# A raw-weight buffer that outlives attention, two weight pieces read early, and plan costs set to measured times

## The chip, the cores and the metric

The kernel runs on one core of a Trainium2 chip. A core has five engines that run their own instruction lists and wait for each other by semaphores: TensorE (PE in the profile, its weight loads PEld), VectorE (DVE), ScalarE (ACT), GpSimd (POOL) and SyncE (SP), which issues most DMAs. The metric is the device time of one execution in microseconds (us). Before the change it was 739.23 us, the median of three runs (738.7 to 740.27).

## The reference

Three parts follow each other. The first is attention over 2 x 8 heads of 768 tokens by 64, in which a query sees only the keys of its own bucket; the bucket is the sign pattern of six random projections. The second is a dense layer over 1536 tokens, and the third sends each token to one of eight experts, 192 tokens each, in the order of the gate's scores.

```python
mask = q_bucket[:, :, :, None] == k_bucket[:, :, None, :]
scores = np.where(mask, scale * q @ k.T, -1e9)     # softmax, then @ v
...
h = x @ w_in                                       # x 1536x512, w_in 512x2048
g = np.maximum(h, 0.0) + alpha * np.minimum(h, 0.0)
x = g @ w_out                                      # w_out 2048x512
...
h = np.maximum(x[mask] @ w1[e], 0.0)               # 192 tokens of each expert
out[mask] = h @ w2[e]
```

w_in and w_out come in 64-bit floating point; every other input is 32-bit.

## The kernel before

**Stages.** Attention fills TensorE until about 225 us. The dense layer, called moe1 in the code, follows until about 530 us and shares its end with the routing of tokens; the experts run until the end. The input of the dense layer, xT, is attention's output transposed, and it has a high part xh and a low part xl, since every product of moe1 is done as three matmuls on rounded halves (low weight by high input, high by low, high by high).

**Weights.** A piece of w_in or w_out is 128 x 512 numbers of 64 bits, read by SyncE as raw words into a buffer of 128 x 1024 words (tile wraw, 512 KB). `turn` makes it usable in five steps: VectorE builds 32-bit numbers in a PSUM bank (tile pscv) in three instructions, b1 (L602), b2 (L605) and b3 (L608); ScalarE copies them to the high half (L613); VectorE subtracts to get the low half (L614). The third step gives the raw buffer back. w_in has 16 pieces, of which 12 are read and turned during attention, and w_out has 16, one for each f below, all of them read and turned in moe1. Two raw buffers, each of one piece, are used in attention; they belong to the pool `stg`, which is closed with attention. moe1 opens two others in its own pool, and reads its four w_in pieces into the space of the next block's input before that is made (tile wx).

**moe1.** Four blocks of 384 tokens, and in each 16 rounds f. A round has twelve matmuls of the first product into the bank psh (L699 to L701); the relu with slope, two passes on ScalarE (L718, L720) and one on VectorE (L722, tile gt); a rounded copy gh on ScalarE (L926) and its remainder gl on GpSimd or VectorE (L930); and twelve matmuls of the second product into the bank psy (L728 to L730), which read gh, gl and the wout halves of f. The high and low part of the next block's input (x_ops, L669 and L672) are made during the block before.

**The order of the work.** Every stage collects its operations in a `Plan`, each with its engine or engines, a cost in us, a priority (a due time), what it comes after, and which buffers of a ring it takes and gives. `Plan.order` simulates engines with these costs, takes at every step the operation that could start first, with the priority as a small weight, and so writes each engine's instruction list once, when the kernel is built. On the chip each engine runs its list in that order. The list therefore depends on the costs and on the constants at the head of the file. Each engine waits in place: if an instruction is not ready, nothing behind it on that engine goes ahead.

**The experts.** For each expert, TensorE picks its tokens' numbers (rp<-tt, L1315), VectorE turns them to an index (L1318), GpSimd issues two gathers (L1383) and the fetches of w1 and w2 (L1365), TensorE transposes the gathered rows (L1413) and makes the products, and GpSimd scatters the results (L1500).

Of the kernel before, what the change touches and what calls it, by code (L numbers as in the profile page):

```python
# [7 lines left out]
F32 = mybir.dt.float32  # L8
# [4 lines left out]
U32 = mybir.dt.uint32  # L13
# [11 lines left out]
XP = 10.89  # L25
RP = 11.53
RB = 19.57
PK0 = -119.54
PK = -106.32
NPL = 4  # L30
NB = 384
# [6 lines left out]
WA = -6.05  # L38
XA = -32.34
TA = 20.0  # L40
TB = 1.5
YA = 0.74
RD = 2.82
HC = 1
HOT = 0
NWA = 12
IN0 = 4.6
IA = -7.85
# [113 lines left out]
class Attn:  # L162
# [353 lines left out]
    def run(s):  # L516
        s.setup()
        s.o_x = {}
        pl = aplan()
        for h in range(2 * NH):  # L520
            s.head(h, pl, h * 6 * SL)
        for i in range(NWA):
            s.m.w_in_ops(pl, i, PO["w"] + i * PO["dw"])
        s.m.consts_ops(pl, s, s.o_x[2])
        s.m.bank0 = s.bank
        pl.emit(s.warm, 1.0, WEND)


class Moe:
# [19 lines left out]
    def consts_ops(s, pl, at, o):  # L549

        nc = s.nc
        T = {}

        def load():
            T["a"] = s.stg.tile([16, 128], F32, name="al16", bufs=1)
            nc.sync.dma_start(out=T["a"], in_=s.alpha.rearrange("(f p) -> f p", p=128))
            nc.sync.dma_start(out=s.wg[:, :, 0:8], in_=s.w_gate.rearrange("(p k) e -> p k e", p=128))

        def tr():
            T["p"] = at.bank("psal")  # L560
            nc.tensor.transpose(T["p"][:, 0:16], T["a"], s.ident[0:16, 0:16])

        def cp():
            nc.vector.tensor_scalar(s.al, T["p"][:, 0:16], -1.0, None, op0=OP.mult)

        o = pl.op({"SP": 1.2}, load, 0.0, [o], dma=0.4)
        o = pl.op({"PE": 0.2}, tr, 0.0, [o], ["B"])
        pl.op({"DVE": 0.1}, cp, 0.0, [o], (), ["B"])
# [8 lines left out]
    def f64_load(s, src):  # L577
        t = s.stg.tile([128, 512, 2], U32, name="wraw", bufs=2)
        s.nc.sync.dma_start(out=t.rearrange("p n two -> p (n two)"), in_=src.bitcast(U32))
        return t  # L580

    def w_in_ops(s, pl, i, at):

        nc = s.nc
        j, k = divmod(i, 4)
        T = {}

        def load():
            T["raw"] = s.f64_load(s.w_in[k * 128:(k + 1) * 128, j * 512:(j + 1) * 512])

        hi, lo = s.wih[j][:, k], s.wil[j][:, k]
        o = pl.op({"SP": 0.45}, load, at, take=["wr"], dma=1.46)
        s.turn(pl, T, o, ["B"], ["wr"], lambda n: s.bank0(n), lambda: hi, lambda: lo, lambda x: at + 3 + x)

# [29 lines left out]
    def w_ops(s, pl, n, src, parts, at, pr, own):  # L624

        nc = s.nc
        T = {}
        bank = ("OA", "OB")[n % 2]

        def load():  # L630
            if own:
                raw = s.xb[1].tile([128, 1536], U32, name="wx", tag=("xh", "xl")[s.nx % 2])[:, 0:1024]
                s.nx += 1
            else:
                raw = s.yp.tile([128, 1024], U32, name="wraw", tag="wr", bufs=2)
            T["raw"] = raw.rearrange("p (n two) -> p n two", two=2)
            nc.sync.dma_start(out=raw, in_=src.bitcast(U32))

        o = pl.op({"SP": 0.45}, load, pr(at - 2.0), take=["XR" if own else "WR"], dma=1.46)
        return s.turn(pl, T, o, [bank], ["XR" if own else "WR"], lambda name: s.bank(name, bank), *parts, lambda x: pr(at + x))  # L640
# [20 lines left out]
    def x_ops(s, pl, blk, k, after, at, w, take=()):  # L661
# [12 lines left out]
        o = pl.op({"ACT": 0.41}, hi, at, after, take)  # L674
        return pl.op({"DVE": 0.47, "POOL": 0.96} if blk else {"DVE": 0.47}, lambda e="DVE": lo(e), at + 0.4 * w, [o])

    def x_init(s, cl):
        s.cl = cl
        s.xb = [cl.enter_context(s.tc.tile_pool(name="xb0", bufs=1))]
        s.xh, s.xl, s.o_xl = {}, {}, {}  # L680
# [66 lines left out]
    def moe1(s, pl, r):  # L747
# [3 lines left out]
        T = {}  # L751
# [37 lines left out]
        def out(e, blk, k):  # L789
            if k % 2 == 0:  # L790
                T["yt", blk] = s.yp.tile([128, 2, NB], F32, name="yt", tag="wr", bufs=2)
# [46 lines left out]
        def wog_ops():  # L838
# [33 lines left out]
            for q in range(4):  # L872
                o_t = []
                for k in range(4):
                    at = (TA + (4 * q + k) * TB) * U
                    o_l = op({"SP": 0.45}, lambda q=q, k=k: load(q, k), at - 2 * U, o_x[1], ["RAW"], dma=1.46)
                    for n, t in enumerate((0.34, 0.6, 0.6)):
# [22 lines left out]
        for blk in range(4):  # L900
# [4 lines left out]
            for f in range(16):  # L905
# [22 lines left out]
                def lo(e, blk=blk, f=f):  # L928
# [3 lines left out]
                for k in range(4):  # L932
                    o_h = [op({"PE": 0.49}, lambda k=k, h=h: h(k), at + 0.1 * k, [o_x[blk][k]] if blk else [o_i[x] for x in (f // 4 * 4 + k,) if x in o_i], [ring] if k == 0 else [],
                              ["X"] if f == 15 and k == 3 and blk < 2 else [], o_h)]
                b = blk < 3
                o = op({"ACT": 0.41}, a1, at + 1.0, o_h, ["GT", "G"] if b else ["GR"], behind=o_free if blk == 3 else [])
                o = op({"ACT": 0.41}, a2, at + 1.1, [o])
                o = op({"DVE": 0.47}, a3, at + 1.15, [o], (), [ring])
                o_a = o
                o = op({"ACT": 0.41}, hi, at + 1.2, [o])  # L940
                o_gl = op({"DVE": 0.85, "POOL": 1.0}, lo, at + 1.3, [o], (), ["GT"] if b else [])
                if b:
                    at = (i + LAG) * U + 0.5
                    for k in range(4):
                        o_y[blk, f, k] = op({"PE": 0.49}, lambda blk=blk, f=f, k=k: y(blk, f, k), at + 0.1 * k,
# [42 lines left out]
        for k in range(4):  # L988
            for f in range(16):
                o = [op({"PE": 0.49}, lambda f=f, k=k: y(3, f, k), at, o_y[3, f], ["L"] if f == 0 else [],  # L990
# [529 lines left out]
def body(ctx, tc, q, k, v, proj, w_in, w_out, alpha, w_gate, w1, w2, cst, w_out_t, out):  # L1520
# [11 lines left out]
    m.x_init(cl)  # L1532
    with ExitStack() as c2:
        m.stg = c2.enter_context(tc.tile_pool(name="stg", bufs=2))
# [56 lines left out]
```

## Time and profile before

| what | value |
|---|---|
| runs | 738.7, 739.23, 740.27 us (median 739.23) |
| the profiled execution | 736.62 us, of which the span on the core is 734.5 us |
| TensorE busy | 709.9 us, 97% of the span |
| VectorE, ScalarE, GpSimd busy | 448.9, 311.3, 257.7 us |
| mean granted clock of TensorE | 0.991 of full speed |

The profile is of one execution, so sums are made against its 736.62 us, which is 2.61 us below the median of the runs. The page lists the busy time of every engine, then the waits by line; a window of the trace gives busy time in a stretch, with the granted clock (1.00 is 2.4 GHz, 0.50 is 1.2 GHz) and the share of time in which the DMA engines worked. In a timeline row the bracket at the end gives the idle time before that instruction on its engine, and the instruction or transfer that ended it. A queue of SyncE is marked SPq.

### The profile page before, as it was taken

The numbers are of one execution on the slowest core, as the hardware profiler recorded it, in microseconds if no ns is written. First come the engines' busy times: TensorE is split into PE (matmuls) and PEld (weight loads), VectorE is DVE, ScalarE is ACT, GpSimd is POOL, SyncE is SP. The second block draws the span as 40 slices with busy tenths as digits, with TensorE's granted clock in tenths as the row PEclk, the third lists the DMA queues.
The fourth block names the chain that finished last, engine by engine and source line by source line (L and its number), as shares of the span: only waits on it lengthen the run. The fifth ranks groups of instructions, "written<-read, shape, count | busy, mean of one in ns | idle before, by whom it ended". The sixth has DMA issues, their size and how long they took to land. (4 is left out here: it accounts for less than half of the span.)

```text
span 734.5 us, 14803 instructions
## 1 busy us (share of the span) xinstructions
PE 709.9 (97%) x6062; PEld 602.2 (82%) x6062; DVE 448.9 (61%) x989; ACT 311.3 (42%) x569; POOL 257.7 (35%) x220
## 2 busy tenths in 40 slices
PE   7999999999988799999999999999999999999996
PEld 6888888888887699999999999898978667666662
DVE  4888988888976989724454533456667565551000
ACT  4677787778743444633353333541021111112110
POOL 2498888889761121100000000005243413323101
PEclk9999999999999999999999999999999999999999
DMA  8455665655205455130223200200667546539201
GB/s 226 99 138 139 152 172 131 175 138 138 45 2 172 141 174 174 37 97 29 87 65 127 86 1 1 76 2 1 217 256 296 220 174 231 200 144 376 98 7 37
DMA packets 33091, 93.27 MB, mean 127 GB/s; under 512 B 4448, under 2 KB 17920, under 8 KB 30720
## 3 DMA queue, kind: packets, MB, share of 16 engines
q1 hardware_dynamic: 28016, 52.08, 24.8%
q0 software_dynamic: 4688, 39.85, 14.8%
q8 instruction: 48, 0.79, 0.4%
q10 hardware_dynamic: 320, 0.40, 0.2%
q14 instruction: 19, 0.16, 0.1%
HBM read 71.86 MB, written 8.65 MB: 110 GB/s over the span
## 5 line engine op out<-in xcount | busy, mean ns | idle before, releaser
L440 POOL TENSOR_TENSOR pl<-p 128x768 f16<-128x768 f32 (+1 forms) x94 | 134.5, 1449 | 35.6 <-ACT p L432 35.4
L334 DVE TENSOR_REDUCE m<-psm 128x1 bf16<-128x768 f32 x96 | 89.8, 956 | 13.9 <-PE psm L328 12.5
L432 ACT ACTIVATE p<-pss 128x768 f32<-128x768 f32 (+1 forms) x98 | 76.4, 797 | 40.2 <-PE pss L426 30.9
L699 PE MATMUL psh<-xh,win 128*128 128x384 f32 x256 | 87.9, 343 | 1.6 <-ACT xT L505 0.9
L701 PE MATMUL psh<-xh,win 128*128 128x384 f32 x256 | 85.9, 335 | 0.0
L700 PE MATMUL psh<-xl,win 128*128 128x384 f32 x256 | 85.7, 335 | 0.0
L930 POOL TENSOR_TENSOR gl<-gt,gh 128x384 fp32r<-128x384 f32 x18 | 19.1, 1066 | 171.4 <-ACT gh L926 169.7
L729 PE MATMUL psy<-gh,wout 128*128 128x384 f32 x192 | 65.2, 340 | 2.8 <-DVE wout L614 2.8
L728 PE MATMUL psy<-gl,wout 128*128 128x384 f32 x192 | 65.9, 343 | 2.0 <-ACT wout L613 2.0
L451 PE MATMUL av<-v,pl 128*128 128x65 f16 x576 | 63.5, 195 | 2.4 <-DVE xt L489 2.4
L730 PE MATMUL psy<-gh,wout 128*128 128x384 f32 x192 | 65.0, 338 | 0.0
L1471 PE MATMUL oa<-xw,ht 128*128 128x512 f32 x128 | 64.7, 598 | 0.0
L722 DVE SCALAR_TENSOR_TENSOR gt<-psh,al,gt 128x384 f32<-128x384 f32 x48 | 29.5, 615 | 55.4 <-ACT psh L720 55.3
L451 PEld LDWEIGHTS <-pl 128*128 128x128 f16 x576 | 53.9, 100 | 11.1 <-issue 11.0
L452 PE MATMUL av<-v,p 128*128 128x65 f16 x576 | 63.1, 195 | 0.0
L453 PE MATMUL av<-v,p 128*128 128x64 f16 x576 | 62.8, 195 | 0.0
L1439 PEld LDWEIGHTS pl<-xg,xw 128*128 128x128 f32 x256 | 42.1, 190 | 19.0 <-issue 18.2
L718 ACT ACTIVATE gt<-psh 128x384 f32<-128x384 f32 x48 | 23.6, 492 | 78.7 <-PE psh L701 78.7
L1439 PEld LDWEIGHTS pl<-xT,xw 128*128 128x128 f32 x256 | 41.9, 190 | 16.8 <-issue 14.6
L424 PE MATMUL pss<-Q,K 128*128 128x384 f32 x192 | 54.8, 364 | 0.9 <-ACT p L432 0.8
L699 PEld LDWEIGHTS psh<-xh,win 128*128 128x128 f32 x256 | 48.1, 188 | 8.2 <-issue 6.1
L452 PEld LDWEIGHTS <-p 128*128 128x128 bf16 x576 | 54.1, 99 | 0.1
(237 smaller groups left out, 1660.8 us busy)
## 6 DMA issues: line engine op xcount, KB each, us to landing
K<-Q SPq DMA_DIRECT2D x45, 192.0 KB, 2.9
wraw<-in_moe_w_out_dram SPq DMA_DIRECT2D x16, 512.0 KB, 3.6
xT<-in_moe_w_out_t_dram SPq DMA_DIRECT2D x16, 512.0 KB, 3.6
wraw<-in_moe_w_in_dram SPq DMA_DIRECT2D x12, 512.0 KB, 4.4
vf<-in_v_dram SPq DMA_DIRECT2D x16, 192.0 KB, 4.2
qk<-in_q_dram SPq DMA_DIRECT2D x15, 192.0 KB, 3.3
qk<-in_k_dram SPq DMA_DIRECT2D x15, 192.0 KB, 3.5
Q<-Q SPq DMA_DIRECT2D x15, 192.0 KB, 3.8
```

Source lines behind the costliest of these rows:

```text
L334: nc.vector.tensor_reduce(T["m"][:, t:t + 1], T["mx", t][:, :, 0:384], axis=AX.XY, op=OP.max, negate=True)
L432: nc.scalar.activation(T["p", c].rearrange("p (a n) -> p a n", a=2)[:, x], T["s", c][:, x, 0:384], AF.Exp, scale=0.125)
L440: (nc.vector if eng == "DVE" else nc.gpsimd).tensor_tensor(T["l", c][:, x], p[:, x], T["h", c][:, x], op=OP.subtract)
L451: nc.tensor.matmul(o[:, t, 0:65], lo[:, sl], vt[:, 0:65], start=(c == 0 and t == 0), stop=False, **kw)
L452: nc.tensor.matmul(o[:, t, 0:65], ph[:, sl], vt[:, 0:65], start=False, stop=False, **kw)
L699: nc.tensor.matmul(o, wl[:, k, ff], s.xh[blk][:, k], start=(k == 0), stop=False)
L700: nc.tensor.matmul(o, wh[:, k, ff], s.xl[blk][:, k], start=False, stop=False)
L701: nc.tensor.matmul(o, wh[:, k, ff], s.xh[blk][:, k], start=False, stop=(k == 3))
L728: nc.tensor.matmul(o, wh, gl, start=first, stop=False, skip_group_check=True)
L729: nc.tensor.matmul(o, wl, gh, start=False, stop=False, skip_group_check=True)
L730: nc.tensor.matmul(o, wh, gh, start=False, stop=last, skip_group_check=True)
L1439: nc.tensor.matmul(T["h", j // 2][:, j % 2], w1[:, k, j * 128:(j + 1) * 128], T["xg"][:, k], start=(k == 0 and j % 2 == 0), stop=(k == 3), ...
```

## The change

The pool `stg` with its two raw buffers is opened with the input blocks and closed with them, in place of being closed with attention. moe1 uses these two buffers in place of two of its own, and so do the tiles yt that carry outputs of the dense layer. A small tile al16 moves to attention's own pool. The new `w_out_early` reads the first two pieces of w_out within attention's plan, and moe1 takes these two as already loaded (`got`). Besides, the costs in moe1's plan rise to measured times: the high and low part of x, the turns of the gate weights, the matmul groups, the relu's passes, gh and gl, and the remainders gl of block 0 go only to GpSimd. Eleven constants that set priorities change too; two of them are shown.

```diff
-PK0 = -119.54
...
+PK0 = -80.645
...
-XA = -32.34
...
+XA = 75.008
...
             s.m.w_in_ops(pl, i, PO["w"] + i * PO["dw"])
+        for f in range(2):
+            s.m.w_out_early(pl, f, PO["w"] + (NWA + f) * PO["dw"])
         s.m.consts_ops(pl, s, s.o_x[2])
...
-            T["a"] = s.stg.tile([16, 128], F32, name="al16", bufs=1)
+            T["a"] = at.sm.tile([16, 128], F32, name="al16", bufs=1)
...
-        t = s.stg.tile([128, 512, 2], U32, name="wraw", bufs=2)
+        t = s.stg.tile([128, 512, 2], U32, name="wraw", tag="wr")
...
         s.turn(pl, T, o, ["B"], ["wr"], lambda n: s.bank0(n), lambda: hi, lambda: lo, lambda x: at + 3 + x)
+
+    def w_out_early(s, pl, f, at):
+
+        def load():
+            s.pre[f] = s.f64_load(s.w_out[f * 128:(f + 1) * 128, :])
+
+        pl.op({"SP": 0.45}, load, at, take=["wr"], dma=1.46)
 
...
             else:
-                raw = s.yp.tile([128, 1024], U32, name="wraw", tag="wr", bufs=2)
+                raw = s.stg.tile([128, 1024], U32, name="wraw", tag="wr")
             T["raw"] = raw.rearrange("p (n two) -> p n two", two=2)
...
 
-        o = pl.op({"SP": 0.45}, load, pr(at - 2.0), take=["XR" if own else "WR"], dma=1.46)
+        def got():
+            T["raw"] = s.pre[n]
+
+        if n < 2 and not own:
+            o = pl.op({"IN": 0.0}, got, pr(at - 2.0), take=["WR"])
+        else:
+            o = pl.op({"SP": 0.45}, load, pr(at - 2.0), take=["XR" if own else "WR"], dma=1.46)
         return s.turn(pl, T, o, [bank], ["XR" if own else "WR"], lambda name: s.bank(name, bank), *parts, lambda x: pr(at + x))
...
 
-        o = pl.op({"ACT": 0.41}, hi, at, after, take)
-        return pl.op({"DVE": 0.47, "POOL": 0.96} if blk else {"DVE": 0.47}, lambda e="DVE": lo(e), at + 0.4 * w, [o])
+        o = pl.op({"ACT": 0.5}, hi, at, after, take)
+        return pl.op({"DVE": 0.54, "POOL": 1.1} if blk else {"DVE": 0.54}, lambda e="DVE": lo(e), at + 0.4 * w, [o])
 
...
         s.xb = [cl.enter_context(s.tc.tile_pool(name="xb0", bufs=1))]
-        s.xh, s.xl, s.o_xl = {}, {}, {}
+        s.xh, s.xl, s.o_xl, s.pre = {}, {}, {}, {}
 
...
-                T["yt", blk] = s.yp.tile([128, 2, NB], F32, name="yt", tag="wr", bufs=2)
+                T["yt", blk] = s.stg.tile([128, 2, NB], F32, name="yt", tag="wr")
...
-                    for n, t in enumerate((0.34, 0.6, 0.6)):
+                    for n, t in enumerate((0.45, 0.7, 0.75)):
...
-                def lo(e, blk=blk, f=f):
+                def lo(e="POOL", blk=blk, f=f):
...
-                    o_h = [op({"PE": 0.49}, lambda k=k, h=h: h(k), at + 0.1 * k, [o_x[blk][k]] if blk else [o_i[x] for x in (f // 4 * 4 + k,) if x in o_i], [ring] if k == 0 else [],
+                    o_h = [op({"PE": 0.52}, lambda k=k, h=h: h(k), at + 0.1 * k, [o_x[blk][k]] if blk else [o_i[x] for x in (f // 4 * 4 + k,) if x in o_i], [ring] if k == 0 else [],
...
-                o = op({"ACT": 0.41}, a1, at + 1.0, o_h, ["GT", "G"] if b else ["GR"], behind=o_free if blk == 3 else [])
-                o = op({"ACT": 0.41}, a2, at + 1.1, [o])
-                o = op({"DVE": 0.47}, a3, at + 1.15, [o], (), [ring])
+                o = op({"ACT": 0.48}, a1, at + 1.0, o_h, ["GT", "G"] if b else ["GR"], behind=o_free if blk == 3 else [])
+                o = op({"ACT": 0.48}, a2, at + 1.1, [o])
+                o = op({"DVE": 0.56}, a3, at + 1.15, [o], (), [ring])
...
-                o = op({"ACT": 0.41}, hi, at + 1.2, [o])
-                o_gl = op({"DVE": 0.85, "POOL": 1.0}, lo, at + 1.3, [o], (), ["GT"] if b else [])
+                o = op({"ACT": 0.5}, hi, at + 1.2, [o])
+                o_gl = op({"DVE": 0.55, "POOL": 1.1} if blk else {"POOL": 1.1}, lo, at + 1.3, [o], (), ["GT"] if b else [])
...
-                        o_y[blk, f, k] = op({"PE": 0.49}, lambda blk=blk, f=f, k=k: y(blk, f, k), at + 0.1 * k,
+                        o_y[blk, f, k] = op({"PE": 0.52}, lambda blk=blk, f=f, k=k: y(blk, f, k), at + 0.1 * k,
...
-                o = [op({"PE": 0.49}, lambda f=f, k=k: y(3, f, k), at, o_y[3, f], ["L"] if f == 0 else [],
+                o = [op({"PE": 0.52}, lambda f=f, k=k: y(3, f, k), at, o_y[3, f], ["L"] if f == 0 else [],
...
+    m.stg = cl.enter_context(tc.tile_pool(name="stg", bufs=2))
...
-        m.stg = c2.enter_context(tc.tile_pool(name="stg", bufs=2))
```

SyncE's queue in attention's last heads, before; K and Q are head 14's and head 15's halves, copied from one buffer to another.

```order
L302 DMA Q_3619<-Q_3618 64x768
L302 DMA K_3877<-Q_3879 64x768
L302 DMA K_3878<-Q_3879 64x768
L302 DMA K_3878<-Q_3880 64x768
L302 DMA Q_3880<-Q_3879 64x768
L637 DMA wraw<-in_moe_w_out_dram 128x1024 x2
L637 DMA wx<-in_moe_w_in_dram 128x1024 x2
L637 DMA wraw<-in_moe_w_out_dram 128x1024 x2
```

The same place after the change, where L581 is the early load.

```order
L302 DMA Q_3619<-Q_3618 64x768
L581 DMA wraw<-in_moe_w_out_dram 128x1024
L302 DMA K_3879<-Q_3881 64x768
L302 DMA K_3880<-Q_3881 64x768
L302 DMA K_3880<-Q_3882 64x768
L302 DMA Q_3882<-Q_3881 64x768
L581 DMA wraw<-in_moe_w_out_dram 128x1024
L646 DMA wx<-in_moe_w_in_dram 128x1024 x2
L646 DMA wraw<-in_moe_w_out_dram 128x1024 x2
L646 DMA wx<-in_moe_w_in_dram 128x1024 x2
```

The first early load stands between the last move of one head and the first move of the next; the second stands behind head 15's last move. The two wraw loads that opened moe1 are gone from that place, and 12 of them stand in a row later.

VectorE's list at the end of attention and the start of moe1, before; the first row is attention's last.

```order
L489 TENSOR_TENSOR xt<-av,r 128x6x64
L722 SCALAR_TENSOR_TENSOR gt<-psh,al,gt 128x384
L602 TENSOR_SCALAR pscv<-wraw 128x512
L605 SCALAR_TENSOR_TENSOR pscv<-wraw,pscv 128x512
L608 SCALAR_TENSOR_TENSOR pscv<-wraw,pscv 128x512
L602 TENSOR_SCALAR pscv<-wraw 128x512
L722 SCALAR_TENSOR_TENSOR gt<-psh,al,gt 128x384
L614 TENSOR_TENSOR wout_4582<-pscv,wout_4582 128x512
L605 SCALAR_TENSOR_TENSOR pscv<-wraw,pscv 128x512
L602 TENSOR_SCALAR pscv<-wx 128x512
L608 SCALAR_TENSOR_TENSOR pscv<-wraw,pscv 128x512
```

And after; L611, L614, L617 and L623 are the four steps b1, b2, b3 and the low half, and L737 is the relu.

```order
L489 TENSOR_TENSOR xt<-av,r 128x6x64
L611 TENSOR_SCALAR pscv<-wraw 128x512 x2
L614 SCALAR_TENSOR_TENSOR pscv<-wraw,pscv 128x512 x2
L617 SCALAR_TENSOR_TENSOR pscv<-wraw,pscv 128x512 x2
L737 SCALAR_TENSOR_TENSOR gt<-psh,al,gt 128x384
L623 TENSOR_TENSOR wout_4585<-pscv,wout_4585 128x512 x2
L611 TENSOR_SCALAR pscv<-wx 128x512
L737 SCALAR_TENSOR_TENSOR gt<-psh,al,gt 128x384
L614 SCALAR_TENSOR_TENSOR pscv<-wx,pscv 128x512
L611 TENSOR_SCALAR pscv<-wx 128x512
L617 SCALAR_TENSOR_TENSOR pscv<-wx,pscv 128x512
```

All three steps of both w_out pieces have moved in front of the first relu; the low halves stand behind it, and then the w_in pieces (wx).

ScalarE's list from attention's last copy, before: gh for the first round is the fourth row.

```order
L505 ACTIVATE xT<-psx 128x768
L718 ACTIVATE gt<-psh 128x384
L720 ACTIVATE psh<-psh 128x384
L926 ACTIVATE gh<-gt 128x384
L718 ACTIVATE gt<-psh 128x384
L720 ACTIVATE psh<-psh 128x384
L718 ACTIVATE gt<-psh 128x384
L613 ACTIVATE wout_4582<-pscv 128x512
L720 ACTIVATE psh<-psh 128x384
L926 ACTIVATE gh<-gt 128x384
```

And after; L733 and L735 are the relu's passes, L622 is a high half and L941 is gh.

```order
L505 ACTIVATE xT<-psx 128x768
L733 ACTIVATE gt<-psh 128x384
L735 ACTIVATE psh<-psh 128x384
L733 ACTIVATE gt<-psh 128x384
L622 ACTIVATE wout_4585<-pscv 128x512 x2
L941 ACTIVATE gh<-gt 128x384
L735 ACTIVATE psh<-psh 128x384
L733 ACTIVATE gt<-psh 128x384
L941 ACTIVATE gh<-gt 128x384
L735 ACTIVATE psh<-psh 128x384
```

The two high halves of wout now stand before the first gh, and the second round's first relu pass before both. TensorE's list, in the same place, has 36 matmuls of the first product ahead of the first group of the second, where it had 42.

## Rows read from the trace of the kernel before

**Rows 1.** The page: busy time, share of the span and instructions of TensorE

```profile
PE 709.9 (97%) x6062; PEld 602.2 (82%) x6062; DVE 448.9 (61%) x989; ACT 311.3 (42%) x569; POOL 257.7 (35%) x220
```

**Rows 2.** Windows: per engine busy us, instructions; then granted clock, DMA share

```profile
240.00:260.00 20.00, 15.16 (x77) 14.08 (x76) 19.85 (x35) 9.66 (x21) 2.78 (x3) 0.94 0.46 148
300.00:400.00 100.00, 100.00 (x603) 94.78 (x602) 47.15 (x84) 40.88 (x87) 3.41 (x3) 1.00 0.26 81
540.00:640.00 100.00, 100.00 (x699) 68.64 (x698) 59.88 (x216) 17.21 (x34) 34.74 (x28) 1.00 0.64 235
```

**Rows 3.** Waits of TensorE in 225 to 500: total us, times, longest

```profile
PE psy L729 <- DVE wout L614: 2.8, 2, 2.0
PE psy L728 <- ACT wout L613: 2.0, 2, 1.2
...
PE psh L699 <- DVE gt L722: 0.7, 1, 0.7
```

**Rows 4.** Timeline of TensorE: start, duration, engine, line, tiles, idle before

```profile
245.38 0.44 PE L729 MATMUL psy<-gh,wout 128*128 128x384 f32 x1 [0.78 <-DVE wout L614]
...
257.50 0.66 PE L729 MATMUL psy<-gh,wout 128*128 128x384 f32 x1 [2.04 <-DVE wout L614]
...
261.08 0.33 PE L699 MATMUL psh<-xh,win 128*128 128x384 f32 x1
...
261.95 0.34 PE L701 MATMUL psh<-xh,win 128*128 128x384 f32 x1
```

**Rows 5.** Windows: five us of the first layer

```profile
255.00:260.00 5.00, 2.91 (x9) 2.69 (x10) 4.95 (x10) 2.19 (x6) 0.00 (x0) 0.76 0.67 211
```

**Rows 6.** Timeline of ScalarE, VectorE and GpSimd where the first layer begins

```profile
224.62 0.81 ACT L505 ACTIVATE xT<-psx 128x768 f32<-128x768 f32 x1 [4.92 <-PE psx L500]
...
228.83 0.62 DVE L722 SCALAR_TENSOR_TENSOR gt<-psh,al,gt 128x384 f32<-128x384 f32 x1 [5.24 <-ACT psh L720]
...
229.95 0.49 ACT L718 ACTIVATE gt<-psh 128x384 f32<-128x384 f32 x1
...
230.08 1.02 POOL L930 TENSOR_TENSOR gl<-gt,gh 128x384 fp32r<-128x384 f32 x1 [9.87 <-ACT gh L926]
...
232.48 0.59 ACT L613 ACTIVATE wout<-pscv 128x512 fp32r<-128x512 f32 x1
...
233.78 0.68 DVE L605 SCALAR_TENSOR_TENSOR pscv<-wraw,pscv 128x512 uint32<-128x512 uint32 x1
...
234.38 0.69 DVE L602 TENSOR_SCALAR pscv<-wx 128x512 uint32<-128x512 uint32 x1
```

**Rows 7.** Timeline of VectorE: three corrections of block 1

```profile
255.34 1.50 DVE L672 TENSOR_TENSOR xl<-xT,xh 128x384 fp32r<-128x384 f32 x3
```

**Rows 8.** Timeline of VectorE, SyncE queue and ScalarE around head 15

```profile
181.25 0.70 DVE L608 SCALAR_TENSOR_TENSOR pscv<-wraw,pscv 128x512 uint32<-128x512 uint32 x1
...
186.68 2.66 SPq L302 DMA_DIRECT2D K<-Q  x3
...
192.94 0.90 ACT L298 ACTIVATE Q<-psc,c 64x768 fp32r<-64x768 f32 x1
```

**Rows 9.** The DMA view: KB each where known, median us to landing

```profile
K<-Q SPq DMA_DIRECT2D x45, 192.0 KB, 2.9
wraw<-in_moe_w_out_dram SPq DMA_DIRECT2D x16, 512.0 KB, 3.6
...
xT<-y_dram,idx POOLq DMA_INDIRECT x16, 3.3
```

**Rows 10.** Tile wraw: us from DMA to landing

```profile
DMA to landing us min/median/max: 3.4/3.6/6.8
```

**Rows 11.** Timeline of GpSimd and TensorE, expert stage

```profile
562.29 0.91 POOL L1383 DMA_INDIRECT xT<-y_dram,idx  x1 [0.30 <-PE rp L1162]
...
566.23 0.31 PE L1413 MATMUL pl<-c,xT 128*128 128x128 f32 x1
...
576.64 0.96 POOL L1365 DMA_INDIRECT xw<-in_moe_w_dram,wi  x1 [3.09 <-DVE S L1245]
```

More of the change, by code (lines that the diff above doesn't have):

```diff
@@ L24 @@
 XWAIT = 0.0005
-XP = 10.89
-RP = 11.53
-RB = 19.57
-PK0 = -119.54
-PK = -106.32
+XP = 11.309
+RP = 16.477
+RB = 85.247
+PK0 = -80.645
+PK = -368.159
 NPL = 4
@@ L37 @@
 LAG = 2
-WA = -6.05
-XA = -32.34
[L40 to L43, printed above, removed]
+WA = -2.128
+XA = 75.008
+TA = 2.631
+TB = 3.193
+YA = -3.871
+RD = 27.672
 HC = 1
@@ L47 @@
 IN0 = 4.6
-IA = -7.85
+IA = -3.738
 SL = 2.15
```

## The prediction

> **What bounds the kernel now.** I read the page's busy times first, then windows along the span, then TensorE's waits stage by stage, and last the timelines around the waits that end late. TensorE is busy 97% of the span [rows 1], and from 300 to 400 and from 540 to 640 it has no idle time and its granted clock is 1.00 (the 2.4 GHz level) [rows 2]: what another engine does there is worth nothing unless TensorE comes to wait for it. Between 240 and 260 it is busy 15.16 of 20 us, at a mean clock of 0.94 [rows 2]. So the time to be had lies where the first layer begins. Of TensorE's waits there (psy is the accumulator of the second product, whose weights are the tile wout) 2.8 us are for VectorE's low half of wout, L614, 2.0 for ScalarE's high half, L613, and 0.7 for a round's relu, L722 [rows 3]. VectorE is the late one: it works 19.85 of those 20 us [rows 2], and yet sat idle 5.24 us just before, until its first relu at 228.83 [rows 6]. That gap exists because no w_out piece can be read before attention's raw buffers are given up.
>
> **What the present waits cost.** The five waits sum to 2.8 + 2.0 + 0.7 = 5.5 us. Two costs come on top that no wait is charged with.
>
> A restart: a matmul that follows a wait doesn't overlap the next (0.44 us at 245.38 [rows 4]), while in a steady row one starts every 0.174 us (five starts from 261.08 to 261.95 [rows 4]). That is 0.27 us for each of five waits, 1.4 us.
>
> The clock: the longest wait, 2.04 us, ends at 257.50, and the 12 matmuls from there take until 261.08 [rows 4], 3.58 us where 12 x 0.174 would be 2.1. The window 255 to 260 has a granted clock of 0.76, a mix of the 1.2 and 2.4 GHz levels, after TensorE had worked only 2.91 of 5 us [rows 5]. Loss 1.5 us. All told 5.5 + 1.4 + 1.5 = 8.4 us.
>
> **The change, part by part.**
>
> *Early load and shared buffer.* Pieces 0 and 1 of w_out land during attention. VectorE's first six conversions then stand ahead of its first relu, where before they stood behind it. They begin when ScalarE's copy L505 ends, 224.62 + 0.81 = 225.43 [rows 6], because it releases a bank and the transposes it reads are TensorE's last work of attention. With six starts 0.60 us apart (233.78 to 234.38 [rows 6], two pieces interleaved) the sixth ends at about 229.1, so the first relu comes at about 229.1 in place of 228.83 [rows 6]. Thus some 3.6 us of VectorE's work moves into its 5.24 us gap, for a delay of 0.25 us. The rest of the queue gets 3.35 us earlier.
>
> *Corrections of the next block.* The four corrections xl of block 1 go from VectorE to GpSimd (and five of the later blocks' too). On VectorE three of them took 1.50 us [rows 7], just ahead of the 2.04 us wait's end: four are worth 2.0 us. Together 5.4 us of lead, against wait sums of 4.8 us on the two wout rows of [rows 3]. Each wait only needs the lead that VectorE has collected by then, so I expect all four to go.
>
> *The new wait at the first psy.* On ScalarE the two high halves of wout now stand before the first gh. ScalarE's relu L718 of round 1 is held by TensorE, at 229.95 as before [rows 6]; then two wout copies at about 0.5 us of pitch (232.48 has 0.59 us duration [rows 6]) make 231.35, gh 0.52 and the link to GpSimd 231.95, gl 1.02 (the row at 230.08 [rows 6]) 232.97. TensorE has 36 matmuls of the first product ahead of it (42 before the change): 36 x 0.174 from 225.5 ends near 231.8, with its last one overhanging to 232.0. So it waits 1.0 us and restarts, 1.3 us: the price of the order. Going through the orders by hand with these durations (an estimate throughout), I find one more wait, 0.3 us for a relu of the ninth group, with restart 0.6. Then nothing: VectorE needs four conversion steps and a relu per round, 4 x 0.60 + 0.62 (228.83 [rows 6]) = 3.0 us, while TensorE needs 24 x 0.174 = 4.2 us. New costs 1.3 + 0.6 = 1.9.
>
> *GpSimd.* The 16 low halves gl of block 0 stay with it alone, and an xl is the same subtraction on the same shape: 20 x 1.02 = 20 us in a block of 16 x 4.2 = 67 us, no bound. But the last two xl of block 1 now stand behind its fifteenth gl, just before their use; from the walk I estimate 0.8 us of cover at the first group of block 1. I take 0, bounds 0 and 3.6 us (second rival).
>
> *SyncE.* The first early load stands in SyncE's queue ahead of head 15's K moves. It waits for VectorE's third step of an earlier piece, 181.25 + 0.70 = 181.95, while the moves issue at 186.68 [rows 8]: 4.7 us of cover, so the wait holds nobody. With 3.6 us to landing (longest 6.8) [rows 9, 10] it lands between 185.6 and 188.8. The three moves issue over 2.66 us, the last some 1.8 us after 186.68, and land 2.9 us later [rows 8, 9], near 191.4; ScalarE's write that needs them is at 192.94 [rows 8], 1.5 us of slack. I take 0, bounds 0 and 0.6 us (if the moves were held back until 188.8). The second early load comes after head 15's moves, where SyncE's queue holds nothing needed before the end of attention.
>
> The Trainium skill, page "DMA: Bandwidth & Descriptors", section "Issuing engines are not separate DMA queues", says that transfers of all issuers run on the same 16 DMA engines and interleave. By that rule a load beside the moves would slow them, and it speaks against the early load. The bound of 0.6 us already holds the case that the moves wait the load out; no run here shows such an overlap yet.
>
> *Plan costs and constants.* They move conversions, corrections and the routing's steps. Where TensorE has no idle time [rows 2] they can only lose. In the routing the first pick stands one round later on TensorE. In the expert stage each gather keeps its place between the same two weight fetches in GpSimd's queue, and most picks stand farther ahead of their transposes. I take 0 with bounds of 0.5 us gain (routing) and 10.3 us loss (third rival).
>
> *Sum.* 8.4 - 1.9 = 6.5 us. The profiled execution of before took 736.62 us (span 734.5 and 2.1 around it) and should come to 730.1; it lies 2.6 us below the median of the runs, 739.23, so on the median's scale 739.23 - 6.5 = 732.7.
>
> **Rivals.**
>
> 1. *The waits come back one by one.* VectorE is busy through 240 to 260 [rows 2]; if a w_in piece or an xl delays it, one wout wait of 2.0 us survives, with its restart 0.3 and clock loss 1.5: gain 2.7, 736.5. For it: VectorE's load in the stretch. Against: the 5.4 us lead.
> 2. *GpSimd's xl is late at block 1.* The first group waits for one gl and one xl, 2 x 1.02 = 2.1 us, and the clock falls as at 257.50, 1.5 us: gain 6.5 - 3.6 = 2.9, 736.3. For it: the small cover. Against: GpSimd is idle half of the block.
> 3. *No change.* The early load is hidden anyway: the rest of VectorE's block 0 work still bounds TensorE and the lead is eaten by later waits: 739.2. For it: every conversion is still done by VectorE. Against: VectorE's 3.0 us a round is below TensorE's 4.2.
> 4. *Slower, in the expert stage.* In it a gather issued at 562.29 lands 3.3 us later [rows 9, 11], 565.6, and TensorE's transposes come at 566.23 [rows 11]: 0.6 us of cover. Should a fetch that waits 3.09 us, as at 576.64 [rows 11], stand ahead of the gather, TensorE waits 2.5 us in each of seven experts, 17.5 us: 739.23 + 17.5 - 6.5 = 750.2; from 0.6 + 6.5/7 = 1.5 us of lateness on it is slower than before. For it: the changed constants act exactly on picks and fetches. Against: the gathers' places in the queue are the same.
>
> **How the numbers follow.** Forecast 0.66, 730.8 to 734.6 by itself (from a gain of all 8.4 us to one of 4.6, with the new costs doubled). Rivals 1 and 2 0.16 together, 736 to 737. No change 0.08. Slower 0.10. About 0.2%, 1.5 us, is what a measurement of this kernel can tell from no change. Faster is then 0.66 + 0.16 = 0.82, same 0.08, slower 0.10. The range 730.8 to 737.2 holds the forecast and rivals 1 and 2, 0.82.
>
> **What would show it.** Right: in the changed kernel's timeline VectorE starts converting at about 225.4; TensorE's first psy matmul comes near 233.0 after a wait of about 1 us for gl; no wait for wout above 0.5 us follows; the granted clock is 1.00 from 240 to 260; TensorE is busy over 19 of those 20 us; attention ends at the same time, so that L505 again begins near 224.6. Wrong: L505 later by more than 0.6 us (the early load disturbs head 15), a wout wait above 1 us (the lead was too small), a wait for xl at the start of block 1, near 290, or waits of TensorE after 540.

## The result, and the profile after

The changed kernel took 731.66 us, median of four runs (731.47 to 735.23), beside 739.75 us for the kernel before (738.7 to 741.93). The ratio is 0.9908, with a 95% interval of 0.9879 to 0.9937: 6.8 us faster, 4.7 to 9.0. The forecast was 732.7, a gain of 6.5. A second set of six runs gave 0.9922 (0.9894 to 0.9951). The profiled execution took 731.55 us, 5.07 us under that of before, with a span of 729.7; the page's first row answers to [rows 1].

```profile
PE 709.6 (97%) x6062; PEld 600.2 (82%) x6062; DVE 446.7 (61%) x977; ACT 311.7 (43%) x572; POOL 266.7 (37%) x229
```

The share of TensorE reads 97% as before; what changed shows only in windows (busy time by engine, then granted clock, DMA share and GB/s), against [rows 2].

```profile
240.00:260.00 20.00, 20.00 (x116) 19.72 (x115) 18.87 (x33) 10.94 (x23) 6.05 (x6) 1.00 0.40 118
...
300.00:400.00 100.00, 100.00 (x606) 95.66 (x603) 49.56 (x85) 39.66 (x85) 8.31 (x7) 1.00 0.30 89
...
540.00:640.00 100.00, 99.69 (x689) 66.32 (x688) 67.49 (x248) 15.73 (x31) 29.12 (x27) 1.00 0.66 245
```

Between 240 and 260 TensorE has no idle time and full clock, where it had 4.84 us idle and 0.94; in 540 to 640 it now waits 0.31 us, where it did not. Its waits from 225 to 300, against [rows 3] (L743 is the first psy matmul, L714 the first psh):

```profile
PE psy L743 <- POOL gl L945: 0.9, 1, 0.9
PE psh L714 <- ACT xT L505: 0.9, 1, 0.9
```

All four waits for wout and the one for the relu are gone, the new one for gl has come, and the wait for L505 is the old one. In the timeline the start of moe1 reads as follows, against [rows 6]:

```profile
224.60 0.81 ACT L505 ACTIVATE xT<-psx 128x768 f32<-128x768 f32 x1 [4.89 <-PE psx L500]
...
225.44 1.29 DVE L611 TENSOR_SCALAR pscv<-wraw 128x512 uint32<-128x512 uint32 x2 [1.87 <-ACT xT L505]
...
229.02 0.61 DVE L737 SCALAR_TENSOR_TENSOR gt<-psh,al,gt 128x384 f32<-128x384 f32 x1
...
230.35 1.08 ACT L622 ACTIVATE wout<-pscv 128x512 fp32r<-128x512 f32 x2
...
231.92 1.00 POOL L945 TENSOR_TENSOR gl<-gt,gh 128x384 fp32r<-128x384 f32 x1 [11.70 <-ACT gh L941]
...
232.97 0.45 PE L743 MATMUL psy<-gl,wout 128*128 128x384 f32 x1 [0.92 <-POOL gl L945]
```

VectorE converts from 225.44 on, in what was its gap; the first relu ends the six conversions at 229.02; TensorE waits once, for the gl behind ScalarE's two copies.

To see where the gain is kept, I took the start of the matmul with the same number in both traces (counting moe1's psh and psy together): the first is 0.02 us earlier, the 151st 6.10, the 214th 6.89, the 1301st, in block 3, 6.91. The last matmul of the experts is 4.82 us earlier. So block 0 gave 6.9 us, blocks 1 to 3 kept them, and routing and experts gave 2.1 back.

### The profile page after: what moved, and what is told of

Its sections match the earlier page's. It is cut to its first block, busy times and chain, and to the rows that moved or that the text cites. A ratio compares the mean times of both kernels' runs of the same rounds, so it can differ in the third digit from the quotient of the medians.

```text
span 729.7 us, 14811 instructions
## 1 busy us (share of the span) xinstructions
PE 709.6 (97%) x6062; PEld 600.2 (82%) x6062; DVE 446.7 (61%) x977; ACT 311.7 (43%) x572; POOL 266.7 (37%) x229
## 5 line engine op out<-in xcount | busy, mean ns | idle before, releaser
L714 PE MATMUL psh<-xh,win 128*128 128x384 f32 x256 | 87.9, 343 | 0.9 <-ACT xT L505 0.9
L743 PE MATMUL psy<-gl,wout 128*128 128x384 f32 x192 | 65.4, 341 | 0.9 <-POOL gl L945 0.9
L745 PE MATMUL psy<-gh,wout 128*128 128x384 f32 x192 | 64.3, 335 | 0.0
L744 PE MATMUL psy<-gh,wout 128*128 128x384 f32 x192 | 64.2, 334 | 0.0
L737 DVE SCALAR_TENSOR_TENSOR gt<-psh,al,gt 128x384 f32<-128x384 f32 x48 | 29.6, 616 | 51.8 <-ACT psh L735 51.8
L733 ACT ACTIVATE gt<-psh 128x384 f32<-128x384 f32 x48 | 23.7, 493 | 78.3 <-PE psh L716 77.6
L714 PEld LDWEIGHTS psh<-xh,win 128*128 128x128 f32 x256 | 48.0, 188 | 7.6 <-issue 6.1
L452 PEld LDWEIGHTS <-p 128*128 128x128 bf16 x576 | 54.1, 99 | 0.1
L453 PEld LDWEIGHTS <-p 128*128 128x128 bf16 x576 | 54.1, 99 | 0.0
```

The lines of the kernel that those rows point to most:

```text
L452: nc.tensor.matmul(o[:, t, 0:65], ph[:, sl], vt[:, 0:65], start=False, stop=False, **kw)
L453: nc.tensor.matmul(o[:, t, 0:64], ph[:, sl], vt[:, 66:130], start=False, stop=(c == 5 and t == 5), **kw)
L714: nc.tensor.matmul(o, wl[:, k, ff], s.xh[blk][:, k], start=(k == 0), stop=False)
L743: nc.tensor.matmul(o, wh, gl, start=first, stop=False, skip_group_check=True)
```

## The experiments

Each kernel ran beside the kernel before on one chip, five rounds unless said.

**The order alone, with late reads.** The order of four engines is unchanged; the two reads go to moe1's buffers, opened after attention. In SyncE's queue they stand behind one read of w_in (wx), where the kernel before had them ahead of both.

```diff
-            s.m.w_out_early(pl, f, PO["w"] + (NWA + f) * PO["dw"])
...
         def got():
-            T["raw"] = s.pre[n]
+            raw = s.yp.tile([128, 1024], U32, name="wraw", tag="wr", bufs=2)
+            T["raw"] = raw.rearrange("p (n two) -> p n two", two=2)
+            nc.sync.dma_start(out=raw, in_=src.bitcast(U32))
```

> The changed kernel with the same order on TensorE, VectorE, ScalarE and GpSimd, but with the raw buffers of before: pieces 0 and 1 of w_out are read into moe1's own buffers once attention has given up its space. Theory (the order of VectorE's list carries the gain, the early read only little): the two reads issue near 222 as before and land near 226, VectorE's first conversion begins at most 1 us later than at 225.44, the first psy matmul at most 1 us later than at 232.97, no wait for wout over 0.5 us follows, and the time is 0 to 1 us over the changed kernel, 731.5 to 732.7. Rival (the early landing carries it): waits for wout of 2 us and more come back, and the time is 735 or more.

Measured: 736.07, ratio 0.9942 (0.9924 to 0.996). My theory fell: the first conversion came at 230.22, not at most 1 us after 225.44. The timeline:

```profile
223.13 0.33 SPq L644 DMA_DIRECT2D wx<-in_moe_w_in_dram  x1
223.51 1.31 SPq L649 DMA_DIRECT2D wraw<-in_moe_w_out_dram  x2
...
230.22 0.69 DVE L609 TENSOR_SCALAR pscv<-wraw 128x512 uint32<-128x512 uint32 x1 [5.44 <-DMA wraw<-in_moe_w_out_dram]
...
235.12 0.44 PE L714 MATMUL psh<-xh,win 128*128 128x384 f32 x1 [4.01 <-DVE gt L737]
```

The reads land 6.6 and 7.0 us after their issue, not the 3.6 I had counted with [rows 9]: four reads of 512 KB leave SyncE within 2.2 us. The kernel before sends four within 1.8 us, too, but these two first. Its two reads, their time to landing, and then the same for this run:

```profile
221.94 0.81 SPq L637 DMA_DIRECT2D wraw<-in_moe_w_out_dram  x2
DMA to landing us min/median/max: 3.6/4.1/4.5
```

```profile
DMA to landing us min/median/max: 6.6/6.8/7.0
```

In the kernel before they landed at 225.56 and 226.84, and the two wx reads behind them took 5.7 and 7.8 us. The Trainium skill, page "DMA: Bandwidth & Descriptors", section "Issuing engines are not separate DMA queues", says that transfers share the 16 DMA engines and interleave; that agrees in so far as reads of one size took 3.6 to 7.8 us with four under way. VectorE stands still behind the conversion, its relu comes late, and TensorE waits 4.0 us for a bank, not for wout as the rival had it; behind that wait the granted clock is at the 1.2 GHz level for 3.4 us. So the new list loses when its data are late. This run does not show that the reads have to be in attention's plan: the same list with the two reads first in SyncE's queue, landing as in the kernel before, was not run.

**The early landing without the order.** The read leaves attention's plan, the buffers stay shared; SyncE still issues the reads during attention.

```diff
-        for f in range(2):
-            s.m.w_out_early(pl, f, PO["w"] + (NWA + f) * PO["dw"])
...
-        if n < 2 and not own:
+        if n < 0 and not own:
```

> The changed kernel without the early read in attention's plan: moe1's plan reads pieces 0 and 1 itself and counts with the time of the read. The buffers live on, so that SyncE's queue can still issue them before attention ends. Theory (order): the first relu stands in front of the first conversion again, VectorE idles until about 228.8, waits of TensorE for wout of 3 us or more in all come back before 265, and the first 214 matmuls of moe1 end 4 to 7 us later than the changed kernel's 264.1; time 735 to 739. Rival (landing): the time stays at 731 to 733.

Measured: 736.75, ratio 0.9943 (0.9922 to 0.9964), inside the theory's range, but not for its reason. TensorE's waits from 225 to 300, but for the one on L505:

```profile
PE psh L712 <- DVE gt L735: 1.9, 3, 1.0
...
PE psy L742 <- DVE wout L621: 0.2, 1, 0.2
```

VectorE again idles 5.24 us and begins with the relu, yet the waits for wout are 0.2 us, not 3. The first 214 matmuls take 40.72 us from the first to the start of the last, beside 45.52 before and 38.65 in the changed kernel. So, with the data landed early in both, the plan's new costs and constants give 4.8 of the 6.9 us, and the early read in the plan, which puts the conversions first, gives 2.1; by the ratios of the runs the first part is 4.2 of 6.8. In this order the four xl are out of VectorE's way and relus stand between the conversions; how much each of the two is worth is not separated.

**The early read with the old costs.** The kernel before with shared buffers, `w_out_early` and `got`, all costs and constants as before.

> The kernel before with the early read and the shared buffers alone, with all costs and constants of before. VectorE's list then also begins with six conversions, but six more stand between one relu and the next and the four xl of block 1 stay on VectorE. Theory (the order made by the measured costs carries most): a relu comes only every 4 x 0.6 x 2 + 0.5 = 5.3 us where TensorE needs 4.2 a round, TensorE waits about 1.2 us for the relu in each of some five rounds, and the time is 734 to 738. Rival (the early read carries it, and the expert stage in the order of before is 1 to 2 us faster than in the changed kernel): 729 to 731.

Measured: 739.74, ratio 0.9985 (0.9958 to 1.0012). The theory's waits came, though its time of 734 to 738 did not: TensorE's waits have this row,

```profile
PE psh L714 <- DVE gt L737: 4.2, 4, 1.5
```

since six conversions and two low halves stand between one relu and the next. This profile also has the half clock described below. The early read alone shows no gain that is clear of noise; the interval allows up to 3.1 us.

**Six more matmuls ahead of the first psy.** Y0 is put behind H's 42nd matmul.

```diff
+        j = o_y[0, 0, 0]
+        o = pl.ops[j]
+        pl.ops[j] = o[:6] + (tuple(o[6]) + tuple(o_h),) + o[7:]
```

> The changed kernel with six more matmuls of the first product (42 in place of 36) ahead of the first psy group on TensorE, all else in the same order. Theory (the wait of 0.92 us for the first gl is open time): the six matmuls, 1.04 us, fill it, the wait falls under 0.1 us, and the time falls by 0.9 to 1.2 us, to about 730.5. Rival (the second group only comes to wait as much, since its gl is as late): no change, 731.5.

Measured: 734.64, ratio 0.9913 (0.9881 to 0.9945), no better than the changed kernel. The profile shows two things. The wait for gl has gone, but TensorE now waits 1.4 us for the bank of the fourth round's psh; and in the window of the start of moe1 the granted clock is 0.50, the 1.2 GHz level:

```profile
PE psh L714 <- DVE gt L742: 1.4, 1, 1.4
...
225.00:230.00 5.00, 4.10 (x14) 3.70 (x13) 3.66 (x6) 0.81 (x1) 0.00 (x0) 0.50 0.39 146
```

In the changed kernel's profile this window has 1.00. TensorE's work is the same there in both, and so is its idle time ahead, 1.83 us before attention's last transposes and 0.90 after. From 226.36 the 36th matmul started at 234.96, 8.6 us after the first in place of 6.25. Hence the next two.

**Filling the seam.** Sixteen 128x128 matmuls on constants, results unused, in that idle time; the changed kernel ran again beside it.

```diff
             T["x"] = s.two("psx")
+            for _ in range(16 if h == 2 * NH - 1 else 0):
+                nc.tensor.matmul(T["x"][:, 0, 0:128], s.ones16, s.ones16, start=True, stop=True)
```

> The changed kernel with 16 small matmuls (128x128, on constants, result not used) on TensorE in its idle 1.83 us before attention's last transposes. Theory (the idle of TensorE between attention and moe1 lets the granted clock fall in some runs, and 6.8 us at half clock there cost 3.4 us): the upper group of runs is gone, the profile's granted clock is 1.00 from 222 on, and the median is that of the changed kernel's lower group, 731 to 732, or 1 to 2 us under its median. Rival (the fall has nothing to do with that idle time): the runs spread as the changed kernel's do, median the same within 0.5 us.

> The changed kernel itself, as the standard for the three kernels beside it. Both theories of the spread expect a ratio to the kernel before near 0.991 and single runs in two groups, about 731.5 and some 3 to 4 us above.

Measured: with the seam filled 731.45 (731.33 to 732.05), ratio 0.9886 (0.9859 to 0.9913); the changed kernel 734.31 (732.48 to 735.16), ratio 0.9922 (0.9894 to 0.9951). Its rows:

```profile
221.74 1.06 PE L500 MATMUL psx<-ones 128*128 128x128 f16 x16
223.64 0.87 PE L502 MATMUL psx<-c,xt 128*128 128x128 f32 x6 [0.84 <-DVE xt L489]
```

The first idle time halves and the runs come together within 0.7 us at the theory's 731 to 732. That does not prove the cause: of nine profiles without the fill three have the half clock at the start of moe1 (six more matmuls, the early read with old costs and the old routing constants), of five with it still one. Nor do runs always come together with it: the four other kernels that have the fill spread over 1.8 to 3.6 us. And there are other places: the changed kernel's second profile, 732.48 us, has full clock at the seam, but its first moe1 matmul comes at 226.49 in place of 225.46, with 0.9 us of that lost before 21 us.

**Both.** Seam filled and 42 matmuls.

> The 16 matmuls and, besides, 42 matmuls of the first product ahead of the first psy group in place of 36. Theory (the wait of 0.92 us for the first gl is open time, and the earlier run that had 42 lost its gain to the half clock at the seam): 0.9 to 1.2 us under the kernel with the 16 matmuls alone, about 730.5, and in the profile the first 214 matmuls of moe1 take 37.5 to 37.9 us from the first on, where the changed kernel took 38.65. Rival (H3 waits for its bank instead): within 0.3 us of the kernel with the 16 matmuls alone.

Measured: 732.56 (731.02 to 733.26), ratio 0.9894 (0.9866 to 0.9922), with the clock at 1.00 at the seam. The rival's mechanism holds, though the time is 1.1 us over the kernel with the 16 matmuls alone and not within 0.3: TensorE's waits now have

```profile
PE psh L716 <- DVE gt L744: 1.3, 1, 1.3
```

and the first 214 matmuls take 38.92 us, no less than 38.65. The fourth round's psh waits for the bank that the second round's relu gives back, and that relu stands as late as gl did.

**Old routing constants.** XP, RP, RB, PK0 and PK as before.

```diff
-PK = -368.159
+PK = -106.32
```

> The changed kernel with the five constants that place the routing and the experts (XP, RP, RB, PK0, PK) as before; moe1's order is that of the changed kernel. Theory (the new places of the first expert's steps give back 2.4 us of the 6.9 gained: its ob product comes 0.3 us before its weights and is split): the first 96 matmuls of the experts take 22.6 to 23.9 us as in the kernels with the old constants, in place of 25.0, and the time is 1 to 2.4 us under the changed kernel's. Rival (the give-back is contention, not order): 25 us again and the same time within 0.5 us.

Measured: 733.75 (731.18 to 735.65), ratio 0.9909 (0.9878 to 0.9939), as the changed kernel's. The first 96 expert matmuls took 23.6 us, as the theory said, but from the 1301st matmul of moe1 to the last expert matmul both take 249.4 to 249.6 us, before 247.3: what the first expert no longer loses goes to waits, which grow by 1.0 us from there on, most of them in the routing. These five constants alone are not what gives back. (The change has twelve constants in all, not eleven.)

**The seam of the kernel before.**

> The kernel before with the 16 small matmuls in TensorE's idle time ahead of attention's last transposes, all else as before. Theory (the half clock at the seam comes and goes in both kernels and blurs the comparison): the runs come together as those of the changed kernel with the same matmuls did, near the profiled 736.6, and against that kernel's 731.45 the change is worth 5.0 to 5.3 us, the difference of the two profiles. Rival (the runs of before spread for another reason, and the change is worth the 6 to 8 us of the medians): the runs still spread over 4 us and their median stays near 739 to 740.

Measured: 739.71 (738.02 to 741.59), ratio 0.9988 (0.9969 to 1.0006). The rival holds in the main: the runs spread over 3.6 us, and their median is in its range. Its profile took 741.59 and has the half clock elsewhere, in the first expert; a row of TensorE, and a window with clock 0.71:

```profile
548.48 0.17 PE L1164 MATMUL rp<-F,ones 128*128 128x8 f16 x1 [1.47 <-DVE F L1160]
```

```profile
550.00:555.00 5.00, 5.00 (x28) 2.11 (x25) 1.07 (x2) 0.06 (x1) 0.00 (x0) 0.71 1.01 360
```

The first 96 expert matmuls took 26.3 us here, 22.6 in the first profile of before. A second profile of the kernel before, of a single execution, asked whether the first was a lucky one:

> The kernel before, profiled a second time. Theory (its first profile was one of its shortest executions, and most others lose 3 to 4 us in the first expert to a wait of TensorE in a routing round and a half clock behind it, as in the profile with the seam filled): time 738 to 741.5, and the second half of the first 96 expert matmuls takes 15 us or more, where the first profile shows 13.6. Rival (the first profile is typical, and the spread is only of the seam): 13.6 us again, and 736.5 unless the clock is halved at the seam.

Measured: 736.76 us, with 22.6 us again. That is the rival's number: the first profile is the kernel undisturbed. It is not a typical execution, since the medians of the runs are 739 to 741. Other executions are up to 9 us longer, and this is one place where such time goes; how often is open.

**Corrections on VectorE.** Seam filled.

```diff
-        return pl.op({"DVE": 0.54, "POOL": 1.1} if blk else {"DVE": 0.54}, lambda e="DVE": lo(e), at + 0.4 * w, [o])
+        return pl.op({"DVE": 0.54}, lambda e="DVE": lo(e), at + 0.4 * w, [o])
```

> The changed kernel with the 16 matmuls at the seam and all corrections xl of blocks 1 to 3 on VectorE, in place of nine of them on GpSimd; they stand as late in VectorE's list as the changed constants put them, behind the conversions. Theory (it is their place, late, that keeps them out of VectorE's way in block 0, not the engine): 0 to 0.4 us from the kernel with the 16 matmuls alone, 731.5, and no wait for wout over 0.5 us. Rival (the engine is what counts, 2.0 us of VectorE's time in block 0, as the prediction had it): a wait for wout or a relu comes back in block 0, 733 to 735.

Measured: 738.87 (737.85 to 740.17), ratio 0.997 (0.995 to 0.999). Both were wrong on the place. Until the 214th matmul it takes 40.24 us, of which about 1.7 are half clock at its start, so this far block 0 runs as the changed kernel's. A wait for wout of 0.86 us comes at 294.47, and then, where block 0 ends, TensorE has these waits among others:

```profile
299.83 0.66 PE L794 MATMUL pst<-c,yt 128*128 128x128 f32 x4 [0.58 <-ACT lt L777]
...
302.52 0.66 PE L794 MATMUL pst<-c,yt 128*128 128x128 f32 x4 [0.69 <-ACT ysb L777]
```

and from the 301st to the 501st matmul it loses 5.1 us. VectorE makes the last three xl only from 302.92 on, so there is no psh of block 1 to put between the steps that carry block 0 out; the changed kernel has psh there. So their late place frees the start of block 0, and with GpSimd they can be late there and still in time for block 1.

**Longer ob groups.** Each end of an ob group costs time in both kernels, so long groups should gain. Seam filled.

```diff
-            for j in range(4):
-                b = [op("PE", 0.86, lambda j=j: tail(j), at + 0.86 * j, [o_t[j // 2], o_t[2 + j // 2]] + f2, ["OB"] if j == 0 else [],
-                        (), b)]
-            return b
+            return [op("PE", 3.44, lambda: [tail(j) for j in range(4)] and None, at, o_t + f2, ["OB"], (), b)]
```

> The changed kernel with the 16 matmuls at the seam and, besides, each expert's eight ob matmuls (64 rows, L1465 before, L1480 after) in one group on TensorE, in place of groups of two between other matmuls: 8 groups in place of 27. Theory (what is given back in the expert stage is lost at the ends of ob groups: 0.47 + 0.52 us for a pair and 0.09 at its start, where a long group takes 0.43 us a matmul, so 0.23 us a group): 19 groups less save 4.4 us, 727.1; if new waits for relu or weights take some of it, 727 to 729.5. Rival (the groups' ends are hidden, or the interleaving hid waits worth as much): 731 to 732.5.

Measured: 726.83 (726.48 to 728.24), ratio 0.9818 (0.9795 to 0.9841). The theory's price of a group's end holds to 0.3 us, and this version beats both kernels: 4.6 us under the 731.45 of the seam alone (5.0 by the ratios). Here TensorE's rows of one group of ob and what follows, first the changed kernel's, where each of its matmuls counts as two records, then this one's:

```profile
566.64 1.08 PE L1480 MATMUL ob<-xw,ht 128*64 128x512 f32 x4
567.65 0.18 PE L1177 MATMUL rp<-F,ones 128*128 128x8 f16 x1
```

```profile
567.35 3.65 PE L1482 MATMUL ob<-xw,ht 128*64 128x512 f32 x16
```

A group of two holds TensorE for 1.0 us, one of eight for 3.6, not 4.0. Added up from each record's start to the next record's, over all 128, ob took 31.5 us before, 32.9 in the changed kernel and 30.0 here; pl, which stands ahead of most groups, took 97.7, 98.3 and 96.3 us from the 1301st matmul of moe1 on. The theory's other half, that the give-back is lost at these ends, does not follow: the changed kernel has 27 groups and the kernel before 26, which is 0.23 us.

## Why the prediction was right, and where it wasn't

**The start of moe1: right to a tenth.** The first conversion was put at 225.43 and came at 225.44, the first relu at 229.1 and came at 229.02, the first psy near 233.0 after a wait of 1.0 us and came at 232.97 after 0.92. The old waits, their restarts and the half clock behind the 2.04 us wait all went. The sum of old costs, 8.4 us, less 1.2 for the one new wait and its restart, is 7.2, and 6.9 was found. The second new wait of 0.3 us did not come, and 1.9 of new costs was 0.7 too much.

**Why VectorE had a gap: wrong.** The prediction says that the 5.24 us are there because no w_out piece can be read before attention's buffers are given up. In that trace the two pieces landed at 225.56 and 226.84, 3.3 and 2.0 us before VectorE's first relu at 228.83, and VectorE did not touch them: the relu stood first in its list. So the gap came from the order, and the early read filled it because the plan, knowing of the data, put the conversions first.

**SyncE: right.** The rows of the changed kernel's SyncE queue, against [rows 8]:

```profile
182.00 0.33 SPq L581 DMA_DIRECT2D wraw<-in_moe_w_out_dram  x1
186.69 2.66 SPq L302 DMA_DIRECT2D K<-Q  x3
```

The moves of head 15 stand where they stood, and L505 begins at 224.60. The read landed at 185.59, before them; so no overlap came about.

**GpSimd's late xl: right.** TensorE has no wait for it at the start of block 1; with the xl as late on VectorE, the end of block 0 lost 5.1 us.

**The shares of the two edits: half right.** The prediction credited the early read with 3.35 us of lead and the xl with 2.0. The runs say 2.1 us for the early read in the plan and 4.8 for the costs and constants, and neither is a sum of leads: the old costs with the early read show no clear gain, the new order with late data 4.3 us.

**Plan costs and constants later on: wrong.** "I take 0" for routing and experts; they gave back 2.1 us of the 6.9, inside the bounds that were set (of which 10.3 us should read 11.0 by the fourth rival's own sum). The prediction looked only at the places of gathers and fetches in GpSimd's queue and at waits. The row that answers for the new wait from 500 on, and TensorE's timeline there, are

```profile
PE ob L1480 <- DMA xw<-in_moe_w_dram,wh: 0.3, 1, 0.3
...
539.46 1.04 PE L1480 MATMUL ob<-xw,ht 128*64 128x512 f32 x2
540.81 1.04 PE L1480 MATMUL ob<-xw,ht 128*64 128x512 f32 x2 [0.31 <-DMA xw<-in_moe_w_dram,wh]
541.78 0.18 PE L1177 MATMUL rp<-F,ones 128*128 128x8 f16 x1
```

This is the first ob group of the first expert. The weights of its second matmul land at 540.67, 1.2 us after its first has begun, so the two run one after the other, and the group takes 2.33 us to the next kind. In every other group of two, in both kernels, the two start within 0.01 us of each other and take 1.01. That is 1.3 us of the 2.1, and the trace calls 0.31 of it a wait; one more group is 0.2, and the rest I have not separated. The place is shown, the cause is not: with the old routing constants this group is whole, and as much is lost elsewhere. Nor do the longer ob groups explain it, since there the first group is split by the same wait (4.90 us, the others 3.59).

**The time.** 732.7 stood against 731.66. On the profile's own scale 730.1 was forecast and 731.55 came, short by the give-back; the medians differ by more than the profiles, because the kernel before more often runs above its profile. So a part of the closeness of the median is chance.

## What to carry to other kernels

An early read is worth what the order makes of it: have the plan know that the data are there, and see that the steps the next engine waits for still come often enough between the conversions. Look for lost time also where the trace shows no wait, by adding up start to start by kind of instruction in both traces; one change found that way gave 4.6 us. When a read comes late, look at its place in the queue, too. And a stretch of idle time between two stages may cost more than itself, in the clock behind it.

## What the runs showed of the hardware

Two ob matmuls (128x64 weights, 512 columns, two records each) run side by side: each takes two records of 0.45 us by itself, but the pair in a long group 0.86 us, 0.43 for each. A group of two takes 1.0 us before another kind starts, and its start comes 0.26 us after a pl matmul ahead of it in place of 0.16; a record of oa, with 128x128 weights, takes 0.43 us and goes on to the next kind after the same 0.43. So these ends, 0.23 us a group, go with the change between the two widths of weights; no run changes the width alone. The Trainium skill, page "TensorEngine Tiling (Array Packing)", section "Key Properties", says that a change of the tiling mode drains TensorE. That agrees with these starts. The prediction did not count such changes in the two orders; between them they differ by one group.

The granted clock went to the 1.2 GHz level for 6.8 us in some executions after 1.83 and 0.90 us of idle time with 0.85 us of work between (six transposes), and not in others of the same instructions. A few us earlier, behind 2.37 us of idle time near 215, 12 of the 14 profiles have 3.4 us at that level; the two that don't are the xl on VectorE and the longer ob groups.

Four reads of 512 KB that one queue sent within 1.8 us landed 3.6, 4.5, 5.7 and 7.8 us after their issue, in the order of the queue.
